# Linear attention with a SwiGLU block: projecting the first two tiles from x less its mean, with 1/std applied later

## The chip, the cores and the metric

The kernel runs on one core of one Trainium2 chip. The metric is the device time of one execution in microseconds (us). Times are medians; the lowest and highest run stand in brackets where they matter. "Excess" means the median of a kernel less the median of the kernel before in the same rounds on the same chip.

The engines are called as in the profile: PE is TensorE (matmuls), PEld its weight loads, DVE is VectorE, ACT is ScalarE, POOL is GpSimd, SP is the engine that issues most DMAs. PSUM banks are the memory into which PE writes; an eviction is the copy of such a bank's content into SBUF, where the other operands lie. A pair such as (min, max) names the two operators that one tensor_scalar instruction applies in turn. Each operator takes a scalar, either a constant in the instruction or, by a pointer, a one-column tile with one value per row.

## The reference

```python
x  = A_x                                  # 1 x 2048 x 512, bf16
xn = (x - mean(x)) / sqrt(var(x) + 1e-5)  # per row
# A: linear attention, 32 heads of 16
q, k, v = split(xn @ wqkv)                # wqkv 512 x 1536
phi = lambda t: where(t > 0, t + 1, exp(t)) + 1e-6
kv  = einsum("bhsd,bhse->bhde", phi(k), v);  z = sum over s of phi(k)
o   = (phi(q) @ kv) / (phi(q) . z + 1e-6)
# B: SwiGLU with 1792 hidden columns
out = x + o @ wo + (silu(xn @ w_gate) * (xn @ w_up)) @ w_down
```

## The kernel before

The 2048 rows are 16 tiles of 128. The first stage (some 60 us) normalizes each tile, transposes it, and projects k and q. phi is computed as max(t, 1e-6) + min(exp(t), 1 + 1e-6): exp on ACT, min on POOL, and the max with the sum on DVE. Instead of projecting v for every row, PE accumulates G = sum over tiles of xn^T phi(k) in four PSUM banks, and applies v's weights once to G.

```python
NWARM = 10                                     # warm-up matmuls, before any data
...
for h, eng in ((0, "sp"), (1, "act")):         # x of tile 0 in two halves
    load(eng, ("x", 0, h), ...)
xload("sp", 1)
wload("act", 1, 0, 2)                          # K weights, first half
wload("sp", 1, 1, 2)                           # K weights, second half
xload("act", 2)
wload("act", 0, 0, 2)                          # Q weights, first half
xload("sp", 3)
wload("sp", 0, 1, 2)                           # Q weights, second half
...
def phi_exp(i, t):
    K.add("act", lambda e: e.activation(ef[:, b - 4, :], banks[b][:, :], ACT.Exp), ...)

def phi_min(i, t):                             # POOL, in place
    K.add("pool", lambda e: e.tensor_scalar(
        out=buf, in0=buf, scalar1=1.0 + 1e-6, scalar2=0.0, op0=ALU.min, op1=ALU.max), ...)

def phi_sum(i, t):
    K.add("dve", lambda e: e.scalar_tensor_tensor(
        out=dst, in0=banks[b][:, :], scalar=1e-6, in1=ef[:, b - 4, :],
        op0=ALU.max, op1=ALU.add), ...)

def gacc(t):
    K.add("pe", [... e.matmul(banks[c][:, :], xn[:, t, c * P:(c + 1) * P], pk[:, t, :], ...)])
...
def divide(t):                                 # later, beside the FFN
    den = tensor_reduce(pz)                    # DVE
    K.add("dve", lambda e: e.tensor_scalar(    # DVE: den += 1e-6
        out=den[:, i, :], in0=den[:, i, :], scalar1=1e-6, scalar2=None, op0=ALU.add), ...)
    rden = reciprocal(den); pq = pq * rden     # DVE
```

(Helper bodies are abbreviated. `pz` is the POOL product of phi(q) and the broadcast z.) The order in which the steps of the 16 tiles are issued is a hand-made list. In the traces each engine takes its own instructions in that order, even where a later one could go first: after the change, POOL normalizes tile 3 at 12.39 us and only then, at 13.14, works on an exp that had been done by 10.34.

Of the kernel before, what the change touches and what calls it, by code (L numbers as in the profile page):

```python
# [6 lines left out]
ACT = mybir.ActivationFunctionType  # L7
# [13 lines left out]
HPG = P // DH  # L21
NH = D // DH

NWARM = 10
NFILL = 3
O_SLOT = {4: 0, 7: 1, 10: 2, 13: 3}
PZ_AT = {9 + 11 * t // 4: t for t in range(16)}
DIV_AT = {j + 1: t for j, t in PZ_AT.items()}
# [79 lines left out]
def bass_parallel_sum__linear_attn_block__swiglu_ffn__prompt_kernel(nc, A_x, A_wqkv, A_wo, B_x, B_w_gate, B_w_up, B_w_down, out):  # L108
# [5 lines left out]
    with contextlib.ExitStack() as es:  # L114
        E = es.enter_context

        def sb(name, shape, dtype):
            return E(nc.sbuf_tensor(name, shape, dtype))

        x_sb = sb("x_sb", [P, NT, D], bf)  # L120
        xn = sb("xn", [P, NT, D], bf)
        xnT = sb("xnT", [P, NDC, S], bf)
        wqkv = sb("wqkv", [P, NDC, 3 * D], bf)
        wo = sb("wo", [P, NG, D], bf)
# [24 lines left out]
        lnv = sb("lnv", [P, NT], f32)  # L149
        rstd = sb("rstd", [P, NT], f32)  # L150
        nm = sb("nm", [P, NT], f32)
        banks = [E(nc.psum_tensor("pb%d" % i, [P, 512], f32)) for i in range(8)]

        def B(i):
# [28 lines left out]


        K.add("act", lambda e: e.preload_act_table_set("natural_log_exp_and_others"))
        for h, eng in ((0, "sp"), (1, "act")):
            load(eng, ("x", 0, h), x_sb[:, 0, h * 256:h * 256 + 256], xin[0:P, h * 256:h * 256 + 256])
        xload("sp", 1)
        wload("act", 1, 0, 2)
        wload("sp", 1, 1, 2)  # L190
        xload("act", 2)
        wload("act", 0, 0, 2)
        xload("sp", 3)
        wload("sp", 0, 1, 2)
        for t in range(4, 16):
            xload("sp", t)

        K.add("pool", lambda e: e.memset(eps5[:, :], 1e-5), w=[("eps5",)])
# [23 lines left out]


        def xk(t):
            return [("x", t)] if t else [("x", 0, 0), ("x", 0, 1)]

        def bn1(t):
            K.add("dve", lambda e: e.bn_stats(stats[:, t, :], x_sb[:, t, :]), r=xk(t), w=[("st", t)])  # L228
# [4 lines left out]
        def rs(t):  # L233
            sl = slice(t, t + 1)
            K.add("act", lambda e: e.activation(lnv[:, sl], mv[:, t, 1:2], ACT.Ln, bias=eps5[:, :], scale=1.0),
                  r=[("mv", t), ("eps5",)], w=[("lnv", t)])
            K.add("act", lambda e: e.activation(rstd[:, sl], lnv[:, sl], ACT.Exp, scale=-0.5),
                  r=[("lnv", t)], w=[("rs", t)])

        def lna_dve(t):  # L240
            K.add("dve", lambda e: e.tensor_scalar(
# [24 lines left out]

        def transp(t, b, lo=0, hi=NDC):
            tb = tview(b, hi - lo)
            K.add("pe", [(lambda e, c=c: e.transpose(tb[:, c - lo, :], xn[:, t, c * P:(c + 1) * P], ident[:, :]))  # L269
                         for c in range(lo, hi)], r=[("xn", t), ("ident",)], w=[B(b)])  # L270

        def evac(t, b, eng="act", lo=0, hi=NDC):
            src = tview(b, hi - lo)
            dst = xnT[:, lo:hi, t * P:(t + 1) * P]
            if eng == "act":
                K.add("act", lambda e: e.activation(dst, src, ACT.Copy), r=[B(b)], w=[("xnT", t, lo)])  # L276
            else:
                K.add("dve", lambda e: e.tensor_copy(dst, src), r=[B(b)], w=[("xnT", t, lo)])

        def xkeys(t):  # L280
            return [("xnT", t, 0), ("xnT", t, 2)] if t == 0 else [("xnT", t, 0)]

        def dmat(t):
            K.add("sp", lambda e: e.dma_start_transpose(out=xnT[:, :, t * P:(t + 1) * P], in_=xn[:, t, :]),
                  r=[("xn", t)], w=[("xnT", t, 0)], dma=True)


        ring = [0]
# [5 lines left out]

        def proj(col, i, t):
            b = nextbank()
            K.add("pe", [(lambda e, c=c: e.matmul(  # L297
                banks[b][:, :], xnT[:, c, t * P:(t + 1) * P], wqkv[:, c, col:col + D],
                start=(c == 0), stop=(c == NDC - 1))) for c in range(NDC)],
                r=xkeys(t) + [("wqkv", i, 0), ("wqkv", i, 1)], w=[B(b)])  # L300
            at[i, t] = b

        def phi_exp(i, t):
            b = at[i, t]
            K.add("act", lambda e: e.activation(ef[:, b - 4, :], banks[b][:, :], ACT.Exp), r=[B(b)], w=[("ef", b - 4)])  # L305

        def phi_min(i, t):
            buf, bkey = ef[:, at[i, t] - 4, :], ("ef", at[i, t] - 4)
            K.add("pool", lambda e: e.tensor_scalar(  # L309
                out=buf, in0=buf, scalar1=1.0 + 1e-6, scalar2=0.0, op0=ALU.min, op1=ALU.max),  # L310
                r=[bkey], w=[bkey])

        def phi_sum(i, t):
            b = at[i, t]
            dst, dkey = ((pk[:, t, :], ("pk", t)) if i else (pq[:, t, :], ("pq", t)))
            K.add("dve", lambda e: e.scalar_tensor_tensor(  # L316
                out=dst, in0=banks[b][:, :], scalar=1e-6, in1=ef[:, b - 4, :], op0=ALU.max, op1=ALU.add),
                r=[B(b), ("ef", b - 4)], w=[dkey])

        def gacc(t):  # L320
            K.add("pe", [(lambda e, c=c: e.matmul(  # L321
                banks[c][:, :], xn[:, t, c * P:(c + 1) * P], pk[:, t, :],
                start=(t == 0), stop=(t == NT - 1))) for c in range(NDC)],
                r=[("xn", t), ("pk", t)], w=[B(c) for c in range(NDC)])


        NZP = 10
# [1 line left out]
        def z_add(half, i):  # L329
            acc, key = zacc[:, half, :], ("zacc", half)  # L330
            t = NZP * half + i
            first, fkey = (pk[:, t - 1, :], ("pk", t - 1)) if i == 1 else (acc, key)
            K.add("dve" if half else "pool",
                  lambda e: e.tensor_tensor(out=acc, in0=first, in1=pk[:, t, :], op=ALU.add),  # L334
                  r=[fkey, ("pk", t)], w=[key])

        def stat(t):
            bn1(t)
            bn2(t)

        steps = {
            "S": stat, "R": rs, "L": lna_dve, "P": lna_pool, "N": nmr, "A": lna_act, "T": lambda t: transp(t, t % 4),
            "E": lambda t: evac(t, t % 4), "V": lambda t: evac(t, t % 4, "dve"), "D": dmat,
            "k": lambda t: proj(D, 1, t), "x": lambda t: phi_exp(1, t), "m": lambda t: phi_min(1, t), "s": lambda t: phi_sum(1, t),
            "q": lambda t: proj(0, 0, t), "y": lambda t: phi_exp(0, t), "n": lambda t: phi_min(0, t), "u": lambda t: phi_sum(0, t), "G": gacc,
            "F": lambda t: keep_busy(t, 256)}

        def run(text):
            for w in text.split():
                steps[w[0]](int(w[1:]))  # L350

        run("""
            S0 R0 S1 L0 R1 L1 S2 T0 E0 F2 T1 V1 R2 L2 k0 k1 x0 m0 S3 T2 S4 x1 m1 E2 R4 s0 q1 R3 L4 k2 x2 N3 A3
            q2 s1 m2 y1 S5 R5 G0 D4 S6 s2 n1 G1 q0 y2 G2 D3 u1 R6 q4 N5 A5 S8 y0 k3 n2 N6 A6 u2 k4 y4 x3 n0 x4
            n4 m3 u0 m4 S13 D5 q3 R8 u4 s3 P8 D6 S7 k5 y3 R13 D8 n3 G3 s4 x5 k6 R7 S9 R9 N7 q6 G4 m5 A7 u3 s5
            S12 x6 q5 G5 N9 m6 S10 A9 y6 s6 y5 q8 R10 D7 k8 N13 n6 R12 u6 y8 G6 n5 x8 D9 u5 A13 k7 x7 S15 S11 k9
            P10 n8 u8 x9 R11 m8 D10 s8 m7 q9 m9 R15 P15 s7 y9 q7 G7 k10 D13 n9 L11 L12 s9 y7 q10 D11 G8 y10 n7
            n10 S14 G9 R14 x10 u7 u9 u10 k11 m10 N14 x11 s10 D15 q13 y13 A14 D12 m11 n13 s11 q11 y11 k12 D14 u13
            x12 m12 k13 k15 n11 x15 m15 u11 G10 x13 m13 s12 G11 q15 q14 y15 n15 s13 s15 k14 x14 m14 y14 q12 s14
            G12 y12 n12 n14 u15 G13 G14 u14 u12 G15  # L360
        """)
        fload("sp", "wg", wg, B_w_gate, 0)
        fload("sp", "wu", wu, B_w_up, 0)
# [31 lines left out]
        def hop(j):  # L395
            C, fc = j // NFC, j % NFC
            K.add("dve", lambda e: e.tensor_tensor(  # L397
                out=hT[:, C % 2, fc, :], in0=banks[gb(j) + 1][:, :], in1=sil[:, j % 2, :], op=ALU.mult),
                r=[B(gb(j) + 1), ("sil", j % 2)], w=[("hT", C % 2, fc)])


        def gt_evac(c, eng):
# [34 lines left out]
        def divide(t):  # L437
            i = t % 2
            K.add("dve", lambda e: e.tensor_reduce(  # L439
                out=den[:, i, :], in_=heads(pz[:, i, :]), axis=mybir.AxisListType.X, op=ALU.add),  # L440
                r=[("pz", i)], w=[("den", i)])
            K.add("dve", lambda e: e.tensor_scalar(
                out=den[:, i, :], in0=den[:, i, :], scalar1=1e-6, scalar2=None, op0=ALU.add),
                r=[("den", i)], w=[("den", i)])
            K.add("dve", lambda e: e.reciprocal(rden[:, i, :], den[:, i, :]), r=[("den", i)], w=[("rden", i)])
            K.add("dve", lambda e: e.tensor_tensor(  # L446
                out=heads(pq[:, t, :]), in0=heads(pq[:, t, :]),
                in1=rden[:, i, :][:, :, None].broadcast_to([P, NH, DH]), op=ALU.mult),
                r=[("pq", t), ("rden", i)], w=[("pq", t)])
            K.add("sp", lambda e: e.dma_start_transpose(  # L450
                out=pk[:, t, :].rearrange("p (g s) -> p g s", g=NG), in_=pq[:, t, :]),
                r=[("pq", t)], w=[("pk", t)], dma=True)
# [113 lines left out]
```

## Time and profile before

| | before |
|---|---|
| time, median of 3 runs | 213.51 us (213.19 to 213.78) |
| span of the profiled execution | 211.6 us |
| PE busy | 208.5 us (99%) |
| POOL min of one tile | 0.612 us, 32 of them |

The two lines of the page that give the chain that ended last, by engine and by line:

```profile
PE 98%; ACT 1%; DVE 0%; issue 0%
PE pb L384 46%; PE pb L467 23%; PE pb L297 13%; PE pb L463 7%; PE pb L321 7%; PE pb L218 2%; PE pb L409 0%; PE pb L457 0%; PE pb L269 0%; ACT ef L305 0%; ACT xnT L276 0%; DVE out_sb L473 0%; PE pb L425 0%
```

The path is PE from end to end. The view of waits lists a single one for PE, 0.8 us at the very start. So the only thing to win is the head, before PE's stream becomes gapless at 9.62 us (by the starts of single matmuls, one per 216 ns from there on). This is PE's timeline of the head (columns: start in us, us, engine, line, operation, output and inputs, count, and what the idle time before it waited for):

```profile
0.84 4.42 PE L218 MATMUL pb<-const-bfloat16-1.0 128*128 128x512 bf16 x10 [0.84 <-PEq L551]
5.25 0.61 PE L269 MATMUL pb<-ident,xn 128*128 128x128 bf16 x4
5.65 0.63 PE L218 MATMUL pb<-const-bfloat16-1.0 128*128 128x256 bf16 x2
6.07 0.42 PE L269 MATMUL pb<-ident,xn 128*128 128x128 bf16 x4
6.54 1.90 PE L297 MATMUL pb<-wqkv,xnT 128*128 128x512 bf16 x8
8.28 0.39 PE L269 MATMUL pb<-ident,xn 128*128 128x128 bf16 x4
8.50 3.02 PE L297 MATMUL pb<-wqkv,xnT 128*128 128x512 bf16 x12
```

L218 is dummy warm-up work, L269 are transposes, L297 are projections: the first useful projection starts at 6.54 us. And this is POOL's share of phi, from the groups of instructions (busy us and mean ns of one; idle before, and who ended it):

```profile
L309 POOL TENSOR_SCALAR ef<-ef 128x512 bf16<-128x512 bf16 x32 | 19.4, 612 | 19.3 <-ACT ef L305 19.1
```

POOL's min takes 0.612 us and POOL waits for ACT, not ACT for POOL. The division of one tile beside the FFN (all engines' timeline around 71 us):

```profile
71.04 0.18 DVE L442 TENSOR_SCALAR den<-den 128x32 f32<-128x32 f32 x1
71.08 1.16 POOL L434 TENSOR_TENSOR pz<-pq,zbc 128x512 f32<-128x512 bf16 x1 [1.93 <-DVE den L439]
...
71.64 1.16 DVE L446 TENSOR_TENSOR pq<-pq,rden 128x512 bf16<-128x512 bf16 x1
```

### The profile page before, as it was taken

The page shows a single profiled execution, that of the slowest core. Times are in us where ns is not written, and L with a number is a line of the kernel's source. Part 1 is how long each engine was busy: PE and PEld are TensorE (multiplying, and loading weights), DVE is VectorE, ACT ScalarE, POOL GpSimd, SP SyncE. Part 2 cuts the span into 40 slices and gives each one's busy share as a digit, 9 for nine tenths or more (in the row PEclk, how much of TensorE's full clock was granted, in tenths as well). Part 3 has the DMA queues.
Part 4 walks back from the last instruction along what each step waited for, and adds up shares of the span by engine and source line. Part 5 has one row for each costly group of instructions (what it writes and reads, how often), then busy time and mean ns, then how long its engine had stood idle before and what let it go on. Part 6 is the DMA issues. An engine that isn't in the chain of part 4 may idle for free.

```text
span 211.6 us, 2659 instructions
## 1 busy us (share of the span) xinstructions
PE 208.5 (99%) x991; PEld 96.2 (45%) x991; DVE 125.3 (59%) x217; ACT 69.7 (33%) x138; POOL 55.6 (26%) x81
## 2 busy tenths in 40 slices
PE   8999999999999999999999999999999999999996
PEld 2544444444544444444444444444444444444455
DVE  3899985546874788664654765573649453532121
ACT  4797974546364333122131313021123122130000
POOL 3257665559923222220210220120204000000000
DMA  6942323499910021102101011101011101100101
GB/s 195 357 97 48 77 57 68 107 382 373 354 51 0 4 49 25 50 0 53 25 25 40 9 29 50 25 25 50 17 35 25 50 16 39 25 25 9 40 25 53
DMA packets 26765, 15.78 MB, mean 75 GB/s; under 512 B 16512, under 2 KB 26752, under 8 KB 26752
## 3 DMA queue, kind: packets, MB, share of 16 engines
q1 hardware_dynamic: 25920, 14.88, 24.9%
q10 hardware_dynamic: 832, 0.72, 1.0%
q8 instruction: 8, 0.13, 0.3%
q14 instruction: 5, 0.04, 0.1%
HBM read 9.70 MB, written 2.10 MB: 56 GB/s over the span
## 4 chain that ended last, share of the span: by engine, by line
PE 98%; ACT 1%; DVE 0%; issue 0%
PE pb L384 46%; PE pb L467 23%; PE pb L297 13%; PE pb L463 7%; PE pb L321 7%; PE pb L218 2%; PE pb L409 0%; PE pb L457 0%; PE pb L269 0%; ACT ef L305 0%; ACT xnT L276 0%; DVE out_sb L473 0%; PE pb L425 0%
## 5 line engine op out<-in xcount | busy, mean ns | idle before, releaser
L392 ACT ACTIVATE sil<-pb 128x512 bf16<-128x512 f32 x56 | 33.3, 597 | 101.2 <-PE pb L384 98.8
L397 DVE TENSOR_TENSOR hT<-pb,sil 128x512 bf16<-128x512 f32 x56 | 38.0, 686 | 36.2 <-PE pb L384 33.4
L384 PE MATMUL pb<-xnT,wu 128*128 128x512 bf16 x224 | 57.8, 379 | 0.0
L384 PE MATMUL pb<-xnT,wg 128*128 128x512 bf16 x224 | 57.8, 379 | 0.0
L467 PE MATMUL pb<-wd,hT 128*128 128x512 bf16 (+1 forms) x238 | 51.2, 367 | 0.0
L434 POOL TENSOR_TENSOR pz<-pq,zbc 128x512 f32<-128x512 bf16 x16 | 18.5, 1161 | 86.1 <-DVE den L439 78.5
L467 PEld LDWEIGHTS pb<-wd,hT 128*128 128x128 bf16 x238 | 23.3, 98 | 25.1
L384 PEld LDWEIGHTS pb<-xnT,wu 128*128 128x128 bf16 x224 | 21.9, 98 | 26.0
L384 PEld LDWEIGHTS pb<-xnT,wg 128*128 128x128 bf16 x224 | 21.9, 98 | 25.9
L473 DVE TENSOR_TENSOR out_sb<-pb,x_sb 128x512 bf16<-128x512 f32 (+1 forms) x17 | 11.2, 660 | 33.5 <-PE pb L467 33.5
L297 PE MATMUL pb<-wqkv,xnT 128*128 128x512 bf16 x128 | 29.6, 379 | 0.1
L309 POOL TENSOR_SCALAR ef<-ef 128x512 bf16<-128x512 bf16 x32 | 19.4, 612 | 19.3 <-ACT ef L305 19.1
L305 ACT ACTIVATE ef<-pb 128x512 bf16<-128x512 f32 x32 | 18.3, 591 | 9.7 <-PE pb L297 9.5
L297 PEld LDWEIGHTS pb<-wqkv,xnT 128*128 128x128 bf16 x128 | 12.3, 98 | 15.2 <-ACT xnT L276 0.8
L446 DVE TENSOR_TENSOR pq<-pq,rden 128x512 bf16<-128x512 bf16 x16 | 17.5, 1092 | 0.6
L463 PE MATMUL pb<-M,pk 128*128 128x512 bf16 (+1 forms) x68 | 16.6, 367 | 0.0
L321 PE MATMUL pb<-pk,xn 128*128 128x512 bf16 x64 | 15.4, 379 | 0.0
L316 DVE SCALAR_TENSOR_TENSOR pk<-pb,ef 128x512 bf16<-128x512 f32 x16 | 10.8, 680 | 4.9 <-POOL ef L309 4.9
L316 DVE SCALAR_TENSOR_TENSOR pq<-pb,ef 128x512 bf16<-128x512 f32 x16 | 10.7, 683 | 3.9 <-POOL ef L309 3.9
L228 DVE BATCH_NORM_STATS2 stats<-x_sb 128x6 f32<-128x512 bf16 x16 | 10.8, 678 | 3.2 <-DMA x_sb<-in_A_x_dram 3.2
L439 DVE TENSOR_REDUCE den<-pz 128x32 f32<-128x512 f32 x16 | 10.8, 675 | 0.0
L334 POOL TENSOR_TENSOR zacc<-zacc,pk 128x512 f32<-128x512 f32 x8 | 10.3, 1292 | 0.6
(46 smaller groups left out, 78.0 us busy)
## 6 DMA issues: line engine op xcount, KB each, us to landing
out_dram<-out_sb SPq DMA_DIRECT2D x15, 128.0 KB, 1.7
x_sb<-in_A_x_dram SPq DMA_DIRECT2D x14, 128.0 KB, 4.3
wg<-in_B_w_gate_dram SPq DMA_DIRECT2D x2, 896.0 KB, 7.8
wu<-in_B_w_up_dram SPq DMA_DIRECT2D x2, 896.0 KB, 9.8
wd<-in_B_w_down_dram SPq DMA_DIRECT2D x2, 896.0 KB, 13.8
wqkv<-in_A_wqkv_dram ACTq DMA_DIRECT2D x2, 256.0 KB, 4.0
wqkv<-in_A_wqkv_dram SPq DMA_DIRECT2D x2, 256.0 KB, 4.7
wqkv<-in_A_wqkv_dram SPq DMA_DIRECT2D x1, 512.0 KB, 7.9
```

Of the source, the lines that this page charges most:

```text
L297: K.add("pe", [(lambda e, c=c: e.matmul(banks[b][:, :], xnT[:, c, t * P:(t + 1) * P], wqkv[:, c, col:col + D], start=(c == 0), stop=(c == ...
L305: K.add("act", lambda e: e.activation(ef[:, b - 4, :], banks[b][:, :], ACT.Exp), r=[B(b)], w=[("ef", b - 4)])
L309: K.add("pool", lambda e: e.tensor_scalar(out=buf, in0=buf, scalar1=1.0 + 1e-6, scalar2=0.0, op0=ALU.min, op1=ALU.max), r=[bkey], w=[bkey])
L316: K.add("dve", lambda e: e.scalar_tensor_tensor(out=dst, in0=banks[b][:, :], scalar=1e-6, in1=ef[:, b - 4, :], op0=ALU.max, op1=ALU.add), ...
L321: K.add("pe", [(lambda e, c=c: e.matmul(banks[c][:, :], xn[:, t, c * P:(c + 1) * P], pk[:, t, :], start=(t == 0), stop=(t == NT - 1))) for ...
L384: fns.append(lambda e, c=c, b=b, w_=w_: e.matmul(banks[b][:, :], w_[:, c, fc * P:(fc + 1) * P], xnT[:, c, C * 512:(C + 1) * 512], start=(c ...
L392: K.add("act", lambda e: e.activation(sil[:, j % 2, :], banks[gb(j)][:, :], ACT.Silu), r=[B(gb(j))], w=[("sil", j % 2)])
L397: K.add("dve", lambda e: e.tensor_tensor(out=hT[:, C % 2, fc, :], in0=banks[gb(j) + 1][:, :], in1=sil[:, j % 2, :], op=ALU.mult), r=[B(gb( ...
L434: K.add("pool", lambda e: e.tensor_tensor(out=pz[:, t % 2, :], in0=pq[:, t, :], in1=zbc[:, :], op=ALU.mult), r=[("pq", t), ("zbc",)], w=[( ...
L446: K.add("dve", lambda e: e.tensor_tensor(out=heads(pq[:, t, :]), in0=heads(pq[:, t, :]), in1=rden[:, i, :][:, :, None].broadcast_to([P, NH ...
L463: fns = [(lambda e, g=g: e.matmul(banks[bank][:, 0:hi - lo], pk[:, t, g * P:(g + 1) * P], M[:, g, lo:hi], start=(g == 0), stop=False)) for ...
L467: fns = [(lambda e, fc=fc: e.matmul(banks[bank][:, 0:hi - lo], hT[:, C % 2, fc, jj * P:(jj + 1) * P], wd[:, fc, lo:hi], start=False, stop= ...
```

## The change

The intent is to start the projections earlier. For tiles 0 and 1, PE projects xc = x - mean, so the transposes need not wait for Ln and Exp of the variance. The factor 1/std is made up later: as the scale of the exp; by working on std * phi(k), that is max(t', std * 1e-6) + std * min(exp, 1 + 1e-6), t' being the unscaled projection; and by giving G the operand xc / var in place of xn. The z sum multiplies tiles 0 and 1 by 1/std on POOL. The division's epsilon becomes std * 1e-6. One warm-up matmul and the fillers go, the loads are reordered, and xn^T of the two tiles (needed by the FFN) comes late, by DMA transpose. The whole order list is new.

```diff
-NWARM = 10
-NFILL = 3
+CENTRED = (0, 1)
+NWARM = 9
...
         xload("sp", 1)
-        wload("act", 1, 0, 2)
-        wload("sp", 1, 1, 2)
-        xload("act", 2)
-        wload("act", 0, 0, 2)
-        xload("sp", 3)
-        wload("sp", 0, 1, 2)
-        for t in range(4, 16):
+        wpart("act", 1, 0, 0, 2)
+        wpart("act", 1, 1, 2, 4)
+        wpart("act", 0, 0, 0, 2)
+        wpart("act", 0, 1, 2, 4)
+        K.add("sp", [], r=[("x", 0, 0)])       # SP waits here for x0's first half
+        for t in range(2, 16):
             xload("sp", t)
...
         def phi_exp(i, t):
+            if t in CENTRED:
+                ... activation(efc[b - 4], banks[b], ACT.Exp, scale=rstd[:, t:t + 1])   # efc is f32
         def phi_min(i, t):
+            if t in CENTRED:
+                ... pool tensor_scalar(out=cbuf, in0=cbuf, scalar1=1.0 + 1e-6,
+                        scalar2=std[:, t:t + 1], op0=ALU.min, op1=ALU.mult)
         def phi_sum(i, t):
+            if t in CENTRED:
+                ... dve scalar_tensor_tensor(..., scalar=flo[:, t:t + 1], op0=ALU.max, op1=ALU.add)
         def gacc(t):
+            src, key = (xg, ("xg", t)) if t in CENTRED else (xn, ("xn", t))
         def z_add(half, i):
+            if half == 0 and i == 1:
+                # two POOL multiplies by rstd, then the add
...
         def divide(t):
+            eps, ekeys = (flo[:, t:t + 1], [("flo", t)]) if t in CENTRED else (1e-6, [])
-                out=den[:, i, :], in0=den[:, i, :], scalar1=1e-6, scalar2=None, op0=ALU.add),
+                out=den[:, i, :], in0=den[:, i, :], scalar1=eps, scalar2=None, op0=ALU.add),
```

(Cut: the new small tensors std, 1/var, flo = std * 1e-6 and their operations, the halved transposes and evictions, and the order list.)

## The prediction

> **What bounds the kernel now.** TensorE. The page gives PE 99% of the 211.6 us span, and the chain of waits is 98% PE. By the starts of single matmuls in the timeline, PE has no gap from 9.62 us to 209.2 us: one 128x512 matmul every 216 ns. A tail of 2.3 us follows in both kernels. Only the first 9.6 us can change. By 9.62 us PE had done 12 transposes (56 ns each when warm) and 12 projection matmuls (3.3 us), as if the stream had begun at 6.3 us. The total moves with this effective start, one for one.
>
> **What the head spends.** Timeline: 10 warm-up matmuls at 427 ns occupy PE to 5.06; the first transpose starts at 5.25, when xn of tile 0 is ready (DVE 4.80 to 5.18, behind Ln and Exp on ACT, 4.13 to 4.66). Two filler matmuls take 0.43 us; tile 0's eviction (ACT, 0.60 us) makes the first projection start at 6.54; 0.25 us more is lost at 9.4 waiting for tile 2's eviction. Spacing halves at about 6.1 us. The Trainium skill (TensorE: Matmul & The Clock Gate, "What's actually happening") says the clock is released after a free-running busy window of 3.4 us; this trace agrees in kind.
>
> **What the change does.** It removes one warm-up (0.43 us) and the fillers (0.43 us). Ln and Exp leave the path to the first transpose; transposes and evictions of tile 0 go in halves. Added: a mean on ACT (about 0.8 us, as its 802 ns normalization), two small Exp per centred tile (0.2 us), r2-scaled operands on DVE (0.4 us each), two late normalizations and DMA transposes, two POOL multiplies for z. The last are off the path: POOL's z sum ended at 59.3 and is consumed at 63.2; the SP queue should issue the FFN weights no later than before (39.2 us).
>
> **Cost on the path (estimates from these durations).** Warm-ups end at 4.63 (next issue), first transposes 4.63 to 5.06, half eviction about 0.4 us, first projection at about 5.5 instead of 6.5. About 0.9 us of it still runs at the half clock, which gives back 0.4 us. If nothing else waited, the effective start would be about 5.8: gain 0.5 us. But the next items are tight: q0's weights (landing 7.1 and 7.8 us in before) are wanted at 7.0 to 7.4; x2 is issued only after x0's half has landed (3.0 us), and its statistics stand on DVE ahead of tile 1's eviction. If the DMA rings share evenly (the skill, DMA: Bandwidth & Descriptors, "Queues, rings and completion order": round-robin; this trace shows it only roughly), q0's second half stalls to about 8; if weights go first, k1 stalls. I expect 0.3 us of the gain to be lost there.
>
> **Prediction.** 213.2 us, 8 in 10 between 212.4 and 214.1. Faster by over 2%: 0.01; within 2%: 0.97; slower by over 2%: 0.02.
>
> **What would show it.** First projection at 5.4 to 5.7 us; a PE gap before the second half of q0, k1 or tile 2's transposes, 0.3 to 1 us in all; saturated PE from about 11 us to the end; PE busy within 1 us; FFN weights issued at 37 to 39 us.
>
> **What would make it wrong.** The idle PE between 5.1 and 5.5 keeps the clock halved one window longer (up to 1.5 us slower); POOL's f32 min stretches the path to the first G; weights landing by 7 us with x2 early (0.6 us faster).

## The result

| | before | after |
|---|---|---|
| time, median of 4 runs | 213.49 us (213.19 to 213.78) | 221.50 us (220.96 to 221.63) |
| span of the profiled execution | 211.6 us | 220.2 us |
| PE busy | 208.5 us | 208.6 us |
| first projection on PE | 6.54 us | 5.53 us |
| mean granted clock | 1.0 | 1.0 |

The ratio is 1.037, with a 95% interval of 1.0348 to 1.0393: 3.7% slower, where "within 2%" had been given a chance of 0.97. A ratio here is the mean time of one kernel's fast runs over that of the other's fast runs of the same rounds, so it is not quite the ratio of the medians in the table. The result is correct, and every run of both kernels had the full clock.

PE did the same work in the same busy time, and the first projection started a microsecond sooner, exactly where it was predicted. All of the loss is PE waiting: span less busy time grew from 3.1 to 11.6 us. The chain that ended last, after:

```profile
PE 83%; DVE 5%; DMA 5%; POOL 3%; issue 2%; ACT 1%; DVEq 0%; POOLq 0%
PE pb L496 42%; PE pb L580 22%; PE pb L373 8%; PE pb L576 6%; PE pb L417 4%; DMA x_sb<-in_A_x_dram 3%; POOL hT L390 2%; DMA xnT<-xn 2%; DVE stats L251 1%; POOL xn L330 1%; DVE hT L509 1%; DVE pk L407 1%; DVE den L555 1%; PE pb L521 0%; PE pb L570 0%
```

A path that was PE alone now runs through an x load, the POOL operation of phi (L390), POOL's normalization (L330), a DMA transpose and the division's add (L555). The view of PE's waits after (engine, line, who was waited for: us in all, times, the longest) sizes them:

```profile
PE pb L417 <- DVE pk L403: 3.1, 2, 1.6
PE pb L373 <- DVE pq L403: 1.1, 1, 1.1
PE pb L373 <- DMA wqkv<-in_A_wqkv_dram: 1.1, 2, 0.6
PE pb L241 <- PEq L664: 0.8, 1, 0.8
PE pb L373 <- DMA xnT<-xn: 0.7, 1, 0.7
PE pb L496 <- DVE hT L509: 0.6, 1, 0.6
PE pb L417 <- DVE pk L407: 0.5, 1, 0.5
PE pb L373 <- ACT hT L350: 0.3, 1, 0.3
```

L417 is G, L373 the projections, L496 the FFN's gate and up, L403 the sum of phi for tiles 0 and 1. The 0.8 us is the start, which before has too; the others add up to 7.4 us; the rest of PE's idle time is in gaps too short for this list. The largest part, 3.1 + 1.1 us, is G and a projection waiting for phi of tiles 0 and 1. The timeline of all engines shows why:

```profile
5.53 1.16 PE L373 MATMUL pb<-wqkv,hT 128*128 128x512 bf16 x4 [0.26 <-ACT hT L350]
...
7.43 0.61 PE L373 MATMUL pb<-wqkv,hT 128*128 128x512 bf16 x2 [0.52 <-DMA wqkv<-in_A_wqkv_dram]
7.71 0.69 DVE L251 BATCH_NORM_STATS2 stats<-x_sb 128x6 f32<-128x512 bf16 x1 [2.20 <-DMA x_sb<-in_A_x_dram]
...
8.62 1.73 PE L373 MATMUL pb<-wqkv,hT 128*128 128x512 bf16 x6 [0.59 <-DMA wqkv<-in_A_wqkv_dram]
...
9.37 0.76 POOL L330 TENSOR_SCALAR xn<-x_sb,nm,rstd 128x512 bf16<-128x512 bf16 x1 [0.40 <-ACT rstd L260]
...
10.12 2.00 POOL L390 TENSOR_SCALAR hT<-hT,std 128x512 f32<-128x512 f32 x1
...
12.16 0.75 DVE L403 SCALAR_TENSOR_TENSOR pk<-pb,flo,hT 128x512 bf16<-128x512 f32 x1 [1.29 <-POOL hT L390]
...
12.39 0.77 POOL L330 TENSOR_SCALAR xn<-x_sb,nm,rstd 128x512 bf16<-128x512 bf16 x1
...
12.96 1.04 PE L417 MATMUL pb<-pk,hT 128*128 128x512 bf16 x4 [1.52 <-DVE pk L403]
...
13.14 2.00 POOL L390 TENSOR_SCALAR hT<-hT,std 128x512 f32<-128x512 f32 x1
...
15.51 3.98 POOL L390 TENSOR_SCALAR hT<-hT,std 128x512 f32<-128x512 f32 x2
...
17.55 0.75 DVE L403 SCALAR_TENSOR_TENSOR pk<-pb,flo,hT 128x512 bf16<-128x512 f32 x1 [1.20 <-POOL hT L390]
...
18.59 0.81 PE L417 MATMUL pb<-pk,hT 128*128 128x512 bf16 x3 [1.57 <-DVE pk L403]
```

Read it backwards from 12.96: G waited for the sum on DVE, which waited for POOL's L390, which took 2.00 us and began only at 10.12 because POOL was normalizing tile 2 until then; and tile 2 was late because its x landed at 7.69 us (5.88 before), as the idle DVE before 7.71 shows. Above it, both halves of the Q weights made PE wait (landings at 7.38 and 8.57 us, 7.05 and 7.81 before). Not all of that is the new order: over all kept traces the first half landed at 6.48 to 7.75 us with the new order of loads and at 6.96 to 8.13 with the old, the second at 7.99 to 8.88 against 7.72 to 8.45. Only x of tile 2 is later in every trace (7.28 to 7.81 against 5.56 to 6.02). The POOL groups give the operation that nobody had costed, and its unchanged sibling:

```profile
L395 POOL TENSOR_SCALAR ef<-ef 128x512 bf16<-128x512 bf16 x28 | 17.2, 622 | 5.7 <-ACT ef L385 5.7
...
L390 POOL TENSOR_SCALAR hT<-hT,std 128x512 f32<-128x512 f32 x4 | 8.0, 2002 | 0.1
```

Four instructions of the same 512 elements per partition take 2.00 us each instead of 0.62. The Trainium skill (Perfetto Trace Analysis, "GPSIMD Engine Instruction") calls POOL spans in a profile unreliable and advises start-to-start spacing; here that agrees: two of them back to back start at 15.51 and 17.48 us, 1.97 us apart.

The last wait is far away, in the FFN. The division of a centred tile, after:

```profile
78.68 1.24 DVE L555 TENSOR_SCALAR den<-den,flo 128x32 f32<-128x32 f32 x1
78.72 1.16 POOL L546 TENSOR_TENSOR pz<-pq,zbc 128x512 f32<-128x512 bf16 x1 [1.92 <-DVE den L551]
...
80.34 0.69 DVE L559 TENSOR_TENSOR pq<-pq,rden 128x512 bf16<-128x512 bf16 x1
```

The add, 0.18 us before, lasts 1.24 us and ends with the POOL product (79.92 and 79.88). The product that follows it on DVE is then free of POOL and takes 0.69 instead of 1.16 us. Adding the three operations gives 2.28 us against 1.69 before, so DVE is 0.6 us later with the FFN's next product, for which PE waits.

The 3.7% thus has four candidates: the POOL operation, the loads, the division's add, and a transpose that lands late. What in the POOL operation costs the time is not visible in the trace: it differs from the old one in three ways (f32 instead of bf16, multiply instead of max, a pointer instead of a constant).

### The profile page after: what moved, and what is told of

Read it like the earlier page. It is cut to its first block, busy times and chain, and to the rows that moved or that the text cites. A ratio compares the mean times of both kernels' runs of the same rounds, so it can differ in the third digit from the quotient of the medians.

```text
span 220.2 us, 2660 instructions
## 1 busy us (share of the span) xinstructions
PE 208.6 (95%) x969; PEld 94.9 (43%) x988; DVE 128.6 (58%) x220; ACT 68.6 (31%) x140; POOL 67.5 (31%) x94
## 4 chain that ended last, share of the span: by engine, by line
PE 83%; DVE 5%; DMA 5%; POOL 3%; issue 2%; ACT 1%; DVEq 0%; POOLq 0%
PE pb L496 42%; PE pb L580 22%; PE pb L373 8%; PE pb L576 6%; PE pb L417 4%; DMA x_sb<-in_A_x_dram 3%; POOL hT L390 2%; DMA xnT<-xn 2%; DVE stats L251 1%; POOL xn L330 1%; DVE hT L509 1%; DVE pk L407 1%; DVE den L555 1%; PE pb L521 0%; PE pb L570 0%
## 5 line engine op out<-in xcount | busy, mean ns | idle before, releaser
L496 PE MATMUL pb<-xnT,wg 128*128 128x512 bf16 x223 | 57.6, 379 | 0.0
L496 PE MATMUL pb<-xnT,wu 128*128 128x512 bf16 x216 | 56.0, 379 | 1.1 <-DVE hT L509 0.6
L496 PEld LDWEIGHTS pb<-xnT,wu 128*128 128x128 bf16 x224 | 21.8, 98 | 27.1 <-DVE hT L509 1.7
L496 PEld LDWEIGHTS pb<-xnT,wg 128*128 128x128 bf16 x224 | 21.9, 98 | 25.8
L373 PE MATMUL pb<-wqkv,xnT 128*128 128x512 bf16 x110 | 25.6, 379 | 2.2 <-DVE pq L403 1.1
L385 ACT ACTIVATE ef<-pb 128x512 bf16<-128x512 f32 x28 | 16.5, 593 | 8.1 <-PE pb L373 8.1
L395 POOL TENSOR_SCALAR ef<-ef 128x512 bf16<-128x512 bf16 x28 | 17.2, 622 | 5.7 <-ACT ef L385 5.7
L373 PEld LDWEIGHTS pb<-wqkv,xnT 128*128 128x128 bf16 x112 | 10.5, 98 | 16.6 <-DVE pq L403 2.2
L559 DVE TENSOR_TENSOR pq<-pq,rden 128x512 bf16<-128x512 bf16 x16 | 16.6, 1035 | 0.6
L417 PE MATMUL pb<-pk,xn 128*128 128x512 bf16 x55 | 13.0, 379 | 0.6 <-DVE pk L407 0.5
L407 DVE SCALAR_TENSOR_TENSOR pq<-pb,ef 128x512 bf16<-128x512 f32 x14 | 9.5, 684 | 3.3 <-POOL ef L395 3.3
L407 DVE SCALAR_TENSOR_TENSOR pk<-pb,ef 128x512 bf16<-128x512 f32 x14 | 9.5, 680 | 2.1 <-POOL ef L395 2.1
L576 PEld LDWEIGHTS pb<-M,pk 128*128 128x128 bf16 x68 | 6.7, 98 | 7.4
```

The costliest lines, as they stand in the source:

```text
L373: K.add("pe", [(lambda e, c=c: e.matmul(banks[b][:, :], src[:, c, t * P:(t + 1) * P], wqkv[:, c, col:col + D], start=(c == 0), stop=(c == ...
L395: K.add("pool", lambda e: e.tensor_scalar(out=buf, in0=buf, scalar1=1.0 + 1e-6, scalar2=0.0, op0=ALU.min, op1=ALU.max), r=[bkey], w=[bkey])
L407: K.add("dve", lambda e: e.scalar_tensor_tensor(out=dst, in0=banks[b][:, :], scalar=1e-6, in1=ef[:, b - 4, :], op0=ALU.max, op1=ALU.add), ...
L417: K.add("pe", [(lambda e, c=c: e.matmul(banks[c][:, :], src[:, t, c * P:(c + 1) * P], pk[:, t, :], start=first, stop=last)) for c in range ...
L496: fns.append(lambda e, c=c, b=b, w_=w_: e.matmul(banks[b][:, :], w_[:, c, fc * P:(fc + 1) * P], xnT[:, c, C * 512:(C + 1) * 512], start=(c ...
L559: K.add("dve", lambda e: e.tensor_tensor(out=heads(pq[:, t, :]), in0=heads(pq[:, t, :]), in1=rden[:, i, :][:, :, None].broadcast_to([P, NH ...
```

## The experiments

All results but one are correct against the reference. The table is followed by each run. Times are medians; each has its own kernel before, so compare the excess.

| run | edit, in short | median us | excess us | ratio, 95% interval |
|---|---|---|---|---|
| after | | 221.50 | 8.0 | 1.037 [1.0348, 1.0393] |
| a_bf16 | exp of tiles 0, 1 kept in bf16 | 220.77 | 7.6 | 1.0358 [1.0325, 1.0391] |
| a_minmax | (min, max) instead of (min, mult), wrong | 216.02 | 2.8 | 1.015 [1.0103, 1.0196] |
| b_mult | before with (min, mult by 1.0) everywhere | 238.63 | 25.4 | one run, state unknown |
| b_mult4 | before with (min, mult by 1.0) in tiles 0, 1 | 216.44 | 3.1 | 1.0147 [1.0132, 1.0161] |
| a_den | constant epsilon in the division | 220.57 | 7.4 | 1.0329 [1.0306, 1.0352] |
| b_ptr | before with a pointer to epsilon in tiles 0, 1 | 214.37 | 1.0 | 1.0048 [1.0035, 1.0061] |
| a_loads | after with before's order of loads | 219.30 | 5.9 | 1.0278 [1.026, 1.0295] |
| fix | std moved into the exp's bias, constant epsilon | 215.25 | 1.9 | 1.009 [1.0073, 1.0107] |
| fix_loads | fix with before's order of loads | 214.81 | 1.4 | 1.0084 [1.0054, 1.0115] |
| best1 | fix_loads with a new order in the head | 214.06 | 0.7 | 1.0034 [1.0011, 1.0057] |
| best2 | another order | 214.44 | 1.1 | 1.0055 [1.0041, 1.0069] |
| fixl_swap | fix_loads, tiles 10 and 14 exchanged | 213.99 | 0.8 | 1.0041 [1.0026, 1.0056] |
| best3 | fixl_swap with another order in the head | 214.18 | 1.0 | 1.0045 [1.0033, 1.0057] |

### The POOL operation: width, pair or pointer

a_bf16 changes the width alone:

```diff
-efc = [hT[:, 0, 2 * b:2 * b + 2, :] ... .bitcast(f32) for b in range(4)]
+efc = [hT[:, 0, 2 * b, :] for b in range(4)]
```

> The changed kernel, with the exp buffer of tiles 0 and 1 in bf16 instead of f32; the POOL operation stays min, then mult by the std pointer. Theory PAIR (the 2.00 us of the POOL operation come from the pair min, mult): it stays at 2.0 us, the PE gaps before the first two G (1.7 us each) and q2 (1.3 us) stay, total 221.5 within 0.7. Theory WIDTH (they come from the f32 data, twice the bytes of before's 0.61 us): it falls to 0.6 to 0.8 us, those gaps fall under 0.5 us, total about 216 (215 to 217.5).

Measured: 220.77 us (220.24 to 221.93). The POOL group of a_bf16:

```profile
L390 POOL TENSOR_SCALAR hT<-hT,std 128x512 bf16<-128x512 bf16 x4 | 8.0, 2000 | 0.1
```

2000 ns, as with f32. The width costs nothing, and the theory that it does, which is also the one the prediction had named as a risk, falls.

a_minmax keeps f32 and all else, and takes away the multiply and its pointer. The result is wrong (relative error 0.026), since std is missing:

```diff
-scalar1=1.0 + 1e-6, scalar2=std[:, t:t + 1], op0=ALU.min, op1=ALU.mult
+scalar1=1.0 + 1e-6, scalar2=0.0, op0=ALU.min, op1=ALU.max
```

> Wrong result on purpose (std is not multiplied in): the changed kernel with f32 kept, but the POOL operation of tiles 0 and 1 is min, then max with immediates, as in the kernel before. Theory PAIR: the operation falls from 2.00 to 0.6 to 0.8 us, total about 216 (215 to 217.5). Theory WIDTH: it stays at 2.0 us, total 221.5 within 0.7.

Measured: 216.02 us (215.80 to 218.10). The POOL group of a_minmax:

```profile
L390 POOL TENSOR_SCALAR hT<-hT 128x512 f32<-128x512 f32 x4 | 2.5, 623 | 0.1
```

The operation is back at 0.62 us in f32, and all three waits of PE for phi of tiles 0 and 1 are gone from the list. The excess falls from 8.0 to 2.8 us: this one operation carries 5.2 us of the loss. Four operations that are 1.4 us longer make 5.5 us, so nearly every added POOL microsecond reached PE.

b_mult separates the pair from the pointer. It was run at another time. It is the kernel before, with a multiply by the constant 1.0, so the result is unchanged:

```diff
-scalar1=1.0 + 1e-6, scalar2=0.0, op0=ALU.min, op1=ALU.max
+scalar1=1.0 + 1e-6, scalar2=1.0, op0=ALU.min, op1=ALU.mult
```

> The kernel before, in which every one of the 32 POOL operations is min, then mult by the immediate 1.0, in bf16, instead of min, then max with 0: same result. Theory PAIR: each takes about 2.0 us instead of 0.61, which POOL cannot hide (32 x 1.4 = 45 us more in a stage of 40 us): total over 230 us. Theory WIDTH, or a theory that the pointer operand costs it: each stays at 0.6 to 0.7 us and the total at 213.5 within 1.

Measured: 238.63 us in one run (mean clock 0.986), so over the 230 us expected, but the excess of 25.4 us is well under the 45 us that the expectation had added up. The reading rests on the duration of the operation, not on this time. The POOL group of b_mult:

```profile
L309 POOL TENSOR_SCALAR ef<-ef 128x512 bf16<-128x512 bf16 x32 | 60.7, 1918 | 6.2 <-ACT ef L305 6.2
```

With bf16, a constant, and no other change, all 32 operations take 1.92 us. So the pair (min, mult) on POOL costs three times the pair (min, max). The 0.08 us that is left up to 2.00 is the most that the pointer can account for. Not every multiply is dear: in the trace of after, (add, mult) with two pointers takes 0.77 us and (mult, add) 0.69 us on POOL. Why this pair is slow is not known from any run here.

b_mult4 asks what the four slow operations cost where the rest of the kernel is as before. The edit is that of b_mult, for t in (0, 1) only.

> The kernel before, with min, then mult by the immediate 1.0 in bf16 in only the four POOL operations of tiles 0 and 1, as the change has them (same result). Theory PAIR as the main cause: four times 1.9 to 2.0 us instead of 0.61 in the first 15 us are enough to open PE gaps like those of the changed kernel (before the first G, before the third q and the second G): 3.5 to 5.5 us more than before, 217 to 219. If the changed kernel's loss needed its other parts (late x2, more POOL work), it is under 1.5 us.

Measured: 216.44 us (216.37 to 216.49), an excess of 3.1 us, a little less than expected. In the changed kernel the same four cost 5.2 us. The difference fits the order there: POOL also normalizes tile 2 just ahead of the first of them and tile 3 between the first two (9.37 and 12.39 us in the timeline above). In the trace of b_mult4 POOL normalizes no tile between its four slow operations. That last step is argued from the timeline, not isolated.

### The division's add

a_den undoes the pointer in the division, in the changed kernel:

```diff
-eps, ekeys = (flo[:, t:t + 1], [("flo", t)]) if t in CENTRED else (1e-6, [])
+eps, ekeys = 1e-6, []
```

> The changed kernel; the epsilon added to den for tiles 0 and 1 is the immediate 1e-6 again instead of a pointer to std*1e-6 (numerically nothing). Theory LOCK (with the pointer, the DVE add loses the shared port to the POOL product that starts 0.04 us after it, and stands until that ends, 1.24 us; with the immediate it wins): the add takes 0.18 us in all 16 tiles, the PE gaps at 81 to 86 us (0.3 and 0.5 to 0.7 us) go, total 0.5 to 1.0 us less than the changed kernel, about 220.7. Rival (the pointer form itself is slow, or the gap has another cause): add stays over 1 us, or the gaps and the total stay.

Measured: 220.57 us (219.74 to 220.66). The group of adds in a_den:

```profile
L555 DVE TENSOR_SCALAR den<-den 128x32 f32<-128x32 f32 x16 | 2.9, 182 | 0.5
```

All 16 adds take 0.18 us and PE's wait for the FFN product is gone from the list. By the ratios the gain is 0.9 us (0.0041 of 213). It is blurred by the clock: three of its four runs had a mean granted clock of 0.992 where after had 1.0. The one run at 1.0 took 219.74, 1.8 us under the median of after.

b_ptr does the reverse in the kernel before, where nothing else disturbs. It adds a one-column tile filled with 1e-6:

```diff
-scalar1=1e-6                                   # for t in (0, 1)
+scalar1=eps6[:, 0:1]
```

> The kernel before, with den's epsilon for tiles 0 and 1 read by a pointer from a tile that holds 1e-6 (same result). Theory LOCK: the add takes 1.2 us for these two tiles and 0.18 for the others, because a pointer operand makes DVE ask for the port after the POOL product has started, and the following product pq*rden falls from 1.15 to 0.7 us, since POOL has then ended; total 0.4 to 1.0 us more, 213.8 to 214.4. Rival (the flo tile or the shifted schedule of the changed kernel made it): 0.18 us, total unchanged.

Measured: 214.37 us (214.02 to 214.60), an excess of 1.0 us. The adds of b_ptr, and PE's one new wait:

```profile
L445 DVE TENSOR_SCALAR den<-den 128x32 f32<-128x32 f32 x14 | 2.5, 181 | 0.5
L445 DVE TENSOR_SCALAR den<-den,eps 128x32 f32<-128x32 f32 x2 | 2.5, 1241 | 0.1
```

```profile
PE pb L386 <- DVE hT L399: 0.6, 1, 0.6
```

The value added is the same; only where it comes from differs, and the add goes from 0.18 to 1.24 us. The Trainium skill (SBUF — State Buffer, "Who interferes with whom") says that DVE and GpSimd share a port pair under an exclusive lock, that a tensor_scalar in a two-port mode and a DVE operation with two SBUF inputs both contend for it, and that whoever issues first blocks the other entirely. The trace agrees for DVE: with the constant, the add is done in 0.18 us although POOL starts beside it; with the pointer, it ends when POOL's 1.16 us product ends. That POOL in turn is held by the short add doesn't show: its product has 1.16 us in both. The rival that a pointer add is slow by itself does not fit another add of after: L289, with a pointer to the negated mean, takes 0.32 us for 512 elements per partition at 5.18 us, when POOL is idle. The add starts only 0.04 us ahead of that product by the records. That the pointer makes DVE ask for the port a moment later than POOL, and so lose, is inferred.

### The loads

a_loads is the changed kernel with the order of loads of the kernel before:

```diff
-        wpart("act", 1, 1, 2, 4)
+        wpart("sp", 1, 1, 2, 4)
+        xload("act", 2)
         wpart("act", 0, 0, 0, 2)
-        wpart("act", 0, 1, 2, 4)
-        K.add("sp", [], r=[("x", 0, 0)])
-        for t in range(2, 16):
+        xload("sp", 3)
+        wpart("sp", 0, 1, 2, 4)
+        for t in range(4, 16):
```

> The changed kernel with the order of loads of the kernel before (the halves of K and Q on both queues, x2 and x3 between them; the wait on x0's half gone). Theory LOADS (the new order brings x2 at 7.7 us instead of 5.9 and Q at 7.4 and 8.6 instead of 7.1 and 7.8, and by way of xn2, which stands ahead of the first min on POOL, delays the first G): x2 lands near 5.9, the first G starts 1.2 to 1.8 us earlier than 12.96, total 1.2 to 1.8 us less than 221.5, about 220. Rival (the POOL chain alone sets the first G, the loads cost nothing on top): total within 0.4 us of 221.5.

Measured: 219.30 us (218.78 to 219.65). The excess falls by 2.1 us, somewhat more than expected: x of tile 2 landed at 5.56 us, and the first G started at 10.97, 2.0 us earlier. As the waits overlap (an earlier tile 2 also moves POOL's chain), this number does not add to that of the POOL operation.

### The corrected change

fix keeps the idea and avoids the slow pair. As std * exp(t) = exp(t + 0.5 ln var), std goes into the exp as a bias, and POOL compares with a pointer to std in the fast pair (the factor 1 + 1e-6 is dropped as immaterial). Tile 1's small std operations also move ahead of its exp:

```diff
-... ACT.Exp, scale=rstd[:, t:t + 1]
+... ACT.Exp, bias=hl[:, t:t + 1], scale=rstd[:, t:t + 1]      # hl = 0.5 * lnv
-scalar1=1.0 + 1e-6, scalar2=std[:, t:t + 1], op0=ALU.min, op1=ALU.mult
+scalar1=std[:, t:t + 1], scalar2=0.0, op0=ALU.min, op1=ALU.max
-eps, ekeys = (flo[:, t:t + 1], [("flo", t)]) if t in CENTRED else (1e-6, [])
+eps, ekeys = 1e-6, []
```

> A correct kernel: the changed one, with std brought in by the exp's bias (exp(r p + ln std)), so that POOL needs only min with the std pointer and max with 0; epsilon of den as an immediate. Loads and order as in the change. Theory PAIR plus LOCK: the POOL operation 0.6 to 0.8 us, den's add 0.18 us, total that of a_minmax less 0.5 to 0.9 us, about 215.2 (214.8 to 215.8). If a pointer in this pair were slow too, it would stay near 220.

Measured: 215.25 us (214.98 to 215.41), as expected. The two repairs, with that move, bring back 6.1 of 8.0 us and the result is correct. The pair (min, max) with a pointer took 0.69 us, against 0.62 with constants, which is a second sign that the pointer was not what cost the 2.00:

```profile
L394 POOL TENSOR_SCALAR hT<-hT,std 128x512 f32<-128x512 f32 x4 | 2.7, 690 | 0.0
```

PE still waits 0.6 us for weights, 0.6 for a transpose, 0.4 for ACT's first eviction and 0.3 for a phi sum.

fix_loads is fix with the edit of a_loads.

> The kernel fix with the order of loads of before. With the POOL cost gone, the head is bound by data: I expect the first projections of Q and tile 1 without waits of over 0.4 us, total 213.6 (213.2 to 214.3), about 1.5 us less than fix: so still not faster than before, since tile 1's transposes stand behind k0 on PE and its eviction behind x2's statistics on DVE. If loads do not matter once POOL is fast: 215.2.

Measured: 214.81 us (214.35 to 216.76), a miss: by the medians the loads' order is worth only 0.4 us here, not the 2 us of a_loads, and the intervals of the two ratios overlap widely, so it may be worth nothing. Weights still cost PE 1.0 us and the transpose 0.8. One of six runs had the clock at 0.992, the 216.76.

best1 changes the order in the head: tile 1's transposes go ahead of k0, its eviction goes to ACT, and k1 precedes q0, whose weights arrive last.

```diff
-... R0 k0 r0 R1 r1 o0 o1 S2 j0 R2 W1 q0 w1 k1 P2 x0 X2 y0 S3 R3 m0 P3 Y2 D3 S4 s0 n0 q1 x1 ...
+... R0 r0 o0 W1 k0 v1 S2 j0 R2 P2 k1 x0 q0 R1 r1 o1 X2 x1 S3 R3 m0 P3 Y2 D3 S4 s0 m1 q1 y0 ...
```

(k, q are projections, W, X transposes, v, w evictions on ACT and DVE, S, R, P statistics and normalization, x, y the exp, m, n the min, s, u the sum.)

> fix_loads with another order of the first items: tile 1's transposes ahead of k0 (into the gap of 0.5 us in which PE waits for tile 0's eviction), its eviction on ACT, k1 ahead of q0. By hand from the measured durations the effective start of the PE stream comes to about 5.6 to 5.9 us against 6.3 of before: total 212.9 (212.6 to 213.3), 0.3 to 0.7 us under before. If the transposes delay the release of the clock, or the late part has its own waits, it stays at 213.2 or above.

Measured: 214.06 us (213.28 to 214.84), a miss by 1.2 us. The wait for weights is gone from its list, but 0.8 us of waiting for DVE's centred tile 1 takes its place. (The list is that of its fastest run, 213.28.)

best2 computes centred tile 1 ahead of tile 1's statistics and moves some small operations:

```diff
-M1 S0 a0 b0 S1 C1 c0 d0 e0 h0 R0 r0 o0 W1 k0 v1 ...
+M1 S0 a0 b0 C1 S1 c0 d0 e0 h0 W1 R0 r0 H0 o0 k0 v1 ...
```

> best1 with three moves in its first 10 us: tile 1's centring ahead of its statistics on DVE (tile 1's transposes waited 0.8 us for it), the second ln std and floor behind the first min on POOL, tile 3's statistics ahead and tile 4's behind the first sum on DVE (the first G waited 0.5 us). By hand the first G starts at about 9.9 instead of 10.26 us and the total is 213.0 (212.6 to 213.7), 0 to 0.8 us under before; with the run-to-run place of the clock's release it may be unclear. If it is above 213.4 the centring of two tiles gains nothing in any order that I found.

Measured: 214.44 us (213.99 to 215.15), a miss again, and above the 213.4 from which, by the expectation, centring two tiles gains nothing in any order found. The wait for tile 1 is gone. Its list has 0.6 us for a transpose, 0.6 for a phi sum, 0.4 for weights and 0.3 for a small ACT operation.

fixl_swap tests the late transpose: in fix_loads, tiles 10 and 14 change places in the order from their projections on, so that the transposed tile that was waited for is used later.

```diff
-... G5 k14 R15 R13 ... n4 k10 D7 x14 ... x10 m14 ...
+... G5 k10 R15 R13 ... n4 k14 D7 x10 ... x14 m10 ...
```

> fix_loads with tiles 10 and 14 exchanged from their projections on (no other edit): PE then takes first the tile whose DMA transpose lands early (24.3 us in fix_loads) instead of the one whose transpose took 4.6 instead of 2.4 us and made PE wait 0.8 us at 27 us. Theory LATE TRANSPOSE (this wait is part of what fix_loads still loses): it shrinks under 0.3 us and the total falls by 0.3 to 0.8 us, to 214.0 to 214.5. Rival: another wait takes its place, total 214.8 within 0.3.

Measured: 213.99 us (213.44 to 214.59), as expected. PE's waits in fixl_swap, of its fastest run:

```profile
PE pb L243 <- PEq L669: 0.8, 1, 0.8
PE pb L422 <- DVE pk L408: 0.5, 1, 0.5
PE pb L378 <- ACT hT L355: 0.3, 1, 0.3
```

The transpose is no longer in the list and by the medians the excess falls by 0.6 us against fix_loads. One transpose still took 4.6 us (issued at 22.65), but PE no longer needed it so soon. So the new order had put a projection too soon behind its transpose. Why single transposes land late (up to 4.7 us after issue in the traces, most at 2.4 to 2.5; the kernel before has one of 3.2) stays open: in fix_loads and after they fall into stretches with DMAs of the two instruction queues, but no run tests that.

best3 joins the exchange with best1's head and a few moves in it. The cut shows the head against that of best2:

```diff
-M1 S0 a0 b0 C1 S1 c0 d0 e0 h0 W1 R0 r0 H0 o0 k0 v1 ... R1 H1 R3 r1 m0 o1 X2 s0 x1 P3 Y2 ...
+M1 S0 a0 b0 S1 C1 c0 d0 e0 h0 R0 r0 H0 o0 W1 k0 v1 ... R1 H1 r1 m0 o1 X2 x1 s0 R3 P3 Y2 ...
```

> best1 with that exchange, and in the first 10 us only two moves: the second floor behind the first min on POOL and tile 4's statistics behind the first sum on DVE. Expected first G at 10.1 instead of 10.26 us; total 213.5 (213.0 to 214.0): even with before. Under 213.2 would be a version that beats both; over 214 would say that the spread of best1 (213.3 to 214.8) has another cause.

Measured: 214.18 us (213.97 to 214.34), a miss, and no better than fixl_swap. No version beat the kernel before by its median.

What the remaining excess of some 0.8 us consists of was not isolated. The profiled run of fixl_swap is no good measure of it, since it took 213.44 us, only 0.2 more than the median of before. It shows one more thing that differs from run to run, the moment at which the half clock of the start ends:

```profile
5.53 1.52 PE L378 MATMUL pb<-wqkv,hT 128*128 128x512 bf16 x4 [0.26 <-ACT hT L355]
```

The same four matmuls took 1.16 us in after, so the half clock lasted longer here. Likewise, the 8 transposes of tiles 0 and 1 and the first 12 projection matmuls took 3.74 us of PE in the fastest run of best1 (213.28), and 4.35 us in the profiled run of best3, which is its median. So a late end of the half clock may be a good part of the excess and of best1's spread; these are single traces, and no run tests it. The other PE waits of best3's trace are 0.7 us for a phi sum, 0.4 for the centred tile 1 and 0.2 for an eviction.

### A side effect: the clock

The profiled run of a_bf16 (221.93 us, mean clock 0.992) shows what 0.992 means. Windows of it (us, busy time and instructions of each engine, granted clock, DMA share, GB/s):

```profile
core 0: us, PE busy (x) PEld busy (x) DVE busy (x) ACT busy (x) POOL busy (x), PEclk, DMA share, GB/s
15.00:18.70 3.70, 1.04 (x4) 0.42 (x6) 2.20 (x4) 0.60 (x1) 3.52 (x4) 0.99 0.07 14
18.70:22.10 3.40, 3.36 (x8) 1.22 (x8) 2.10 (x5) 1.50 (x6) 3.19 (x6) 0.50 0.06 14
22.10:26.00 3.90, 3.90 (x19) 1.76 (x18) 3.67 (x9) 2.73 (x8) 2.99 (x7) 1.00 0.27 55
```

After a stretch in which PE was busy for only 1.04 of 3.70 us, the clock was halved for one stretch of 3.4 us: 8 matmuls in it, where at 216 ns some 16 fit. That costs about 1.7 us. The idle time came in pieces of 1.1 and 1.6 us. This is no rule, though: after had the same 1.04 of 3.70 us (14.86 to 18.56) and kept the full clock. A mean clock of 0.992 was seen in seven timed runs, three of a_den and one each of a_bf16, a_minmax, a_loads and fix_loads, and in no run of the kernel before, so it goes with the changed kernels' spread. (The traces of a_minmax and fix_loads, taken at the full clock, have no PE wait over 1.0 us.) It is not the cause of the result: all four runs of after had a clock of 1.0.

## Why the prediction was wrong

The mechanism at the start was right, and so was the location of the waits for loads. The sum lacked its largest term.

- **Right.** First projection predicted at 5.5, seen at 5.53 us. PE busy within 1 us: 208.5 and 208.6. The z sum stayed off the path: PE never waited for it. Gaps before the second half of q0 were named and came. The risk of the clock staying halved one window longer did not come true in after (it may have in other versions, see best3).
- **The step that failed: "Cost on the path".** It followed the path up to "first projection at about 5.5 instead of 6.5" and the loads, and then concluded "gain 0.5 us", less 0.3. The operations behind the projection, exp, min, sum, up to the first G, were charged nothing, as if POOL's new operation took the 0.61 us of the old one. It takes 2.00, and nearly all of the difference reached PE: 5.2 us (a_minmax). The prediction had said it would cost operations from durations in the trace, but the trace of before has no (min, mult) on POOL, so it had none for this one. The risk "POOL's f32 min stretches the path to the first G" named the right engine and the right consequence for the wrong reason: f32 costs nothing (a_bf16), the pair does (b_mult). And it was given no size, although the range of 212.4 to 214.1 depended on it.
- **A mis-sized term: the loads.** "I expect 0.3 us of the gain to be lost there" rested on an either-or: the Q weights late or x2 late. Both came late in after (q0's halves 0.3 and 0.8 us, x2 1.8 us later than before), though over all traces only x2 is later throughout. PE's waits for weights alone were 1.1 us. The Trainium skill (DMA: Bandwidth & Descriptors, "Queues, rings and completion order") says that the engines go round-robin between the queues that have work; that agrees with both queues being slowed, though no run here isolates it. Undoing the order gave 2.1 us in the changed kernel and 0.4 us after the repair, which is not clear of noise, presumably because x2's lateness had acted mostly through POOL's slow chain, which the trace of after suggests and no run isolates.
- **Not foreseen: the division's pointer.** About 0.6 us of waiting and 0.9 to 1.0 us of time by the ratios (a_den, b_ptr), from an instruction of 32 elements whose cost the diff shows as nothing.
- **Not foreseen: a late transpose,** 0.7 us, an effect of the new order (fixl_swap).
- **Wrong without cost.** "Saturated PE from about 11 us to the end" failed: waits appear up to 34 us, and at 82 to 86 us. The FFN weights were issued at 46.7 instead of 37 to 39 us, and PE never waited for them.
- **What remains.** With all four repaired, the change still loses about 0.8 us, where the prediction saw a gain of 0.2 to 0.5. Waits for phi sums (0.5 to 0.7 us) and a half clock that ends late in some runs are seen, and how the 0.8 us splits stays open. That the head can be no faster because weights and x arrive only at 6 to 8 us is argued, not shown.

## What to carry to other kernels

An operation that the old trace does not contain has no duration yet: a change of the second operator, or of a constant to a pointer, makes a new instruction, and it should be measured alone, or given the widest range, before it is placed on a chain. When a change starts the first work earlier, follow the path to the first place where another engine's result is needed, not only to the first matmul. And where a scale has to be applied, see whether an operation that is there already takes it for almost nothing: here the bias of the exp (0.77 instead of 0.68 us on ACT) replaced the multiply on POOL (0.69 instead of 2.00 us), and brought back most of the loss.

## What the Trainium skill lacked or had wrong

- GPSIMD Engine Reference, "4.1 Engine selection", says of elementwise work on GpSimd that one-input operations run roughly at line rate. That depends on the pair of operators: on 128x512 elements (min, max) took 0.61 to 0.62 us (0.69 with a pointer), (mult, add) 0.69, (add, mult) 0.77, but (min, mult) 1.92 us with a constant and 2.00 with a pointer, and alike in bf16 and f32.
- TensorE: Matmul & The Clock Gate, "Why this matters for your kernels", asks for no idle gaps over about 3 us. Here the clock was halved for 3.4 us after gaps of only 1.1 and 1.6 us, with PE busy for 1.04 of the 3.70 us ahead of it (a_bf16), so gaps under 3 us were no protection; in the profiled run of after, with the same busy share in the same place, the clock was not halved. What decides between the two is not shown.
- SBUF — State Buffer, "Who interferes with whom", describes the lock, but says nothing of scalar operands by pointer: the same add of 128x32 took 0.18 us with a constant and 1.24 us with a pointer, beside the same POOL product (b_ptr). That the pointer decides who gets the lock is inferred.
